# A block-sparse attention kernel with a feed-forward part: value products over the whole array, and the first V transfers regrouped

## The chip, the cores and the metric

One Trainium2 chip, and one of its cores. The metric is device time in microseconds of one execution. The kernel before has a median of 317.98 us over three runs (316.88 to 318.97). The profiled execution took 316.81 us, of which 315.0 us lie between its first and its last instruction (the span).

The engines are named as in the profile: PE (matrix products; PEld is its loading of weights), DVE (vector), ACT (scalar), POOL (GpSimd), SP (the engine that only issues transfers here). "SPq" and the like are the engines' own queues of instructions.

## What is computed

```
q, k, v: (4, 8, 768, 64) fp32; sampled_blocks: (24, 3) int64; block = 32, 24 blocks
scores = q k^T / 8, kept where |qblock - kblock| <= 1, or qblock or kblock is 0 or 23,
         or kblock is one of sampled_blocks[qblock]; elsewhere -1e9
attn   = softmax(scores);  y = attn v
x      = y laid out as (4*768, 8*64)
h      = x @ w_in            (512 -> 2048)
out    = (h * sigmoid(beta * h)) @ w_out     (2048 -> 512), fp32
```

## The kernel before

**Attention.** The 22 inner query blocks of each of the 4 batches are taken two at a time: 11 pairs per batch, 44 pairs `n`. A pair works on 8 key blocks per query block: 3 sampled, block 0, 3 neighbours (the block itself and one on each side), block 23. Query block 0 and 23, which see all keys, are done apart ("global rows", `gs`, `gm`, `ge`, `gn`, `gt`, `gav`).

For a pair, in order: `kg` (POOL) copies the 3+3 sampled key blocks into `KG`, at addresses read from `offP`; `kn` (POOL or DVE) copies the neighbours' keys; `sc` (PE, lines 658 and 668) makes the scores in row- and column-tiled products; `mx` (DVE, L679) and `ex` (ACT, L687) do maximum and exponential; `rc`, `nrm` (POOL, L699) divide by the sum; `tp` (PE, L711) transposes the probabilities with 8 products of 128x128; `ptv` (DVE, L715) moves them to `PT`; `av` (PE, L727) multiplies with the pair's value rows in `VG`; `xv` (DVE or ACT, lines 259 and 261) moves the result, transposed, to `xT`.

In `av` the 128 rows of a stationary operand are 4 key blocks of V (c = 0: sampled blocks and block 0; c = 1: neighbours and block 23), and its 64 columns one head of 64. Two heads `u` lie side by side in the array as two column tiles. That is 2 query blocks x 4 head pairs x 2 x 2 = 32 products with 32 columns moving each, into 256 columns of one PSUM bank.

**Value rows.** `VG` has four buffers; a pair's buffer holds 2 x 2 x 512 values on 128 partitions. V in fp16 is first written to a table in DRAM (`VT`, transfers `vtab`), and the buffers are filled from it by transfers on SP's queue (`vg`, L627): the neighbours' rows (96 partitions, 192 KB), the sampled blocks (six of 32 KB, at addresses read by `vv`), and blocks 0 and 23 (two of 64 KB, on partitions 96 to 127) where the buffer is fresh. Of the first four pairs the sampled rows come from PE instead: `pick` (L638) multiplies V, already on chip, with a selection matrix, and `pickv` moves the result. For the first pairs of a later batch, `vres` copies the rows of blocks 0 and 23 from another buffer on chip.

**Weights.** w_in and w_out come in 8 transfers of 256 KB each on POOL's queue (`win`, `wout`, L461 and L467). A tiny POOL copy, `touch` (L447), reads the first half of batch 0's V and holds them back until it has landed. The transfers of batch 1's V, K and Q follow the last of them on the same queue (L491).

**Feed-forward part.** The tokens are cut into 8 groups of 256 or 512. Per group: 16 tiles `h` (PE, L868, four 128x128 products each), `tanh` (ACT, L874), `stt` (DVE, L879), then `y` (PE, L896). They fill PE between the pieces of attention. The first group needs all of w_in and the results of the first four pairs.

**The order** of every engine's instructions is fixed before launch: class `Plan` simulates the engines with the durations given to `add(...)` and always takes the ready task with the lowest `prio`. So a changed duration or dependency can change the order everywhere. A task's name is its kind and its pair or group.

**Start.** Batch 0's K, Q and V come in six transfers of 768 KB on SP's queue; DVE casts K and Q to fp16, PE transposes them (L508), ACT and DVE move them to `KT` and `QT`; `vperm0` (DVE) makes V's fp16 rows. The sampled block numbers come first (`sbl`, L291), with a step of two words, since they are int64; a mask is built from them on DVE.

Of the kernel before, what the change touches and what calls it, by code (L numbers as in the profile page):

```python
# [22 lines left out]
class Task:  # L23
    def __init__(self, name, eng, dur, emit, deps=(), prio=0.0, lat=0.0,
                 opens=(), closes=(), moe=False, dma=0.0, slack=0.0, hw=0, bulk=None):
        self.on = {eng: dur} if isinstance(eng, str) else dict(eng)
        self.name, self.eng, self.dur, self.emit = name, None, None, emit
        self.deps = [d for d in deps if d is not None]
        self.prio, self.lat = prio, lat
        self.opens, self.closes, self.moe, self.dma = opens, closes, moe, dma  # L30
        self.slack, self.hw, self.bulk = slack, hw, bulk
        self.kind = name.rstrip("0123456789.")
        self.end = None


class Plan:


    HOP = 0.18

    def __init__(self, n_banks, moe_banks):
# [9 lines left out]
    def run(self):  # L51
# [17 lines left out]
        lanes = [0.0] * 8  # L69
        issued = 0  # L70

        bank_free = [(0.0, i) for i in range(self.n_banks)]
# [15 lines left out]
        while done < len(tasks):  # L88
            progress = False
            for e in engines:  # L90
# [3 lines left out]
                for t in waiting[e]:  # L94
                    if ready_at[t] > now + 1e-9:
                        continue
                    if len(t.on) > 1:
                        cost = {o: max(free[o], now) + d + BIAS.get((t.kind, o), 0.0)
                                for o, d in t.on.items()}
                        if cost[e] > min(cost.values()) + 1e-9:  # L100
                            continue
                    if t.bulk is not None and ring_at > now + t.bulk + 1e-9:
                        continue
                    if t.opens:
                        n_ok = sum(1 for f, _ in bank_free if f <= now + 1e-9)
                        if n_ok < len(t.opens):
                            continue
                        if t.moe and attention_left and held_moe + len(t.opens) > self.moe_banks:
                            continue
                    if best is None or t.prio < best.prio:  # L110
                        best = t
# [3 lines left out]
                for other in t.on:  # L115
                    waiting[other].remove(t)
                t.eng, t.dur = e, t.on[e]
                if t.opens:
                    bank_free.sort()
                    for name in t.opens:  # L120
                        _, i = bank_free.pop(0)
                        self.bank[name] = i
                        if t.moe:
                            held_moe += 1
                            moe_owner.add(name)
                    if not t.moe:
                        attention_left -= 1
# [55 lines left out]
def kernel(  # L183
# [11 lines left out]
    nc = tc.nc  # L195
# [19 lines left out]
    def sb(name, shape, dt=FP16):  # L215
        return pool.tile(shape, dt, name=name)

    NKG, NVG, NP, NPT, NT, NO, NG = 3, 4, 3, 2, 3, 3, 2
    NSEL = 4
    PK, GSB = 0.6, 5  # L220

    SR, SG0, SN, SG1 = 0, 3, 4, 7
# [14 lines left out]
    KG = [sb(f"KG{i}", [P, 2, NHP, 8 * BLK]) for i in range(NKG)]  # L237
    VG = [sb(f"VG{i}", [P, 2, 2, D_MODEL]) for i in range(NVG)]
    PP = [sb(f"PP{i}", [P, 2, 2, 8 * BLK]) for i in range(NP)]
# [30 lines left out]

    sbl = sb("sbl", [1, NB, 3], I32)
    ctx_nc = nc
# [14 lines left out]
    def emit_sbl():  # L287
        src = sampled_blocks.tensor
        import dataclasses
        h = dataclasses.replace(src, shape=[NB, 6], dtype=I32)  # L290
        nc.scalar.dma_start(out=sbl, in_=bass.AP(tensor=h, offset=0, ap=[[0, 1], [6, NB], [2, 3]]))  # L291
    t_sbl = add("sbl", "ACT", 0.5, emit_sbl, prio=-200, dma=0.3, hw=1)

# [11 lines left out]
    def emit_idx():  # L305
        V = nc.gpsimd
        V.tensor_copy(out=sf, in_=sbl[:, 1:NB - 1, :])
        for t, m in ((offP, 16.0), (offV, 32.0)):
            V.tensor_scalar(out=t[:, :, 0:6], in0=sf[:, :, :].rearrange("o (p g) r -> o p (g r)", g=2),
                            scalar1=m, scalar2=1.0, op0=ALU.mult, op1=ALU.mult)  # L310
# [120 lines left out]
    for i, (nm, t, dst) in enumerate((("K", k, RK), ("Q", q, RQ), ("V", v, None))):  # L431
        for f in range(2):
            tl = add(f"ld{nm}0.{f}", "SP", 0.47, lambda i=i, t=t, f=f: nc.sync.dma_start(
                out=stage_half(i, f) if i < 2 else v_stage[:, f * HH:(f + 1) * HH, :],
                in_=src6(t, 0, f * HH, HH)), prio=-80 + i * 2 + f, dma=2.0, hw=1)
            if nm == "V":
# [12 lines left out]

    tch = touch(w_in_sb[0:1, 0, 0:1], v_stage[0:1, 0, 0:1], v0ld[0], -58)  # L450

# [6 lines left out]
    for c in range(4):  # L458
        for f in range(2):
            ps = slice(64 * f, 64 * f + 64)  # L460
            t_win.append(add(f"win{c}.{f}", "POOL", 0.6, lambda c=c, ps=ps: nc.gpsimd.dma_start(  # L461
                out=w_in_sb[ps, c, :], in_=w_in_r[c, ps, :]),
                deps=[tch], prio=-50 + 0.2 * c + 0.1 * f, dma=1.3, bulk=THR))
    for c in range(4):
        for f in range(2):
            ps = slice(64 * f, 64 * f + 64)
            t_wout.append(add(f"wout{c}.{f}", "POOL", 0.6, lambda c=c, ps=ps: nc.gpsimd.dma_start(  # L467
                out=w_out_sb[ps, 4 * c:4 * c + 4, :].rearrange("x i m -> x (i m)"), in_=w_out_r[c, ps, :]),
                deps=[tch], prio=-49 + 0.2 * c + 0.1 * f, dma=1.3, bulk=THR))

# [6 lines left out]
    for b in range(B):  # L477
# [24 lines left out]
        for nm, s16, dstT, tr, ev in (("K", RK, KT, trK, evK), ("Q", RQ, QT, trQ, evQ)):  # L502
            for hp in range(NHP):
                def emit_tr(nm=nm, s16=s16, b=b, hp=hp):
                    o = bank16((nm, b, hp))
                    for j in range(J):
                        for u in range(2):
# [3 lines left out]
                                identity=identity, tile_position=(0, u * D))  # L511
                tr[b, hp] = add(f"tr{nm}{b}.{hp}", "PE", 0.36, emit_tr, deps=[ld[nm, b, hp], t_ident],
                                prio=pr + hp, lat=0.2, opens=((nm, b, hp),))
# [34 lines left out]
    for n, (b, p) in enumerate(order_pairs):  # L548
# [5 lines left out]
        first_v = n < NVG or order_pairs[n - NVG][0] != b  # L554
        head_v = p == 0 or n < NSEL
        kt32 = KT[b % 2][:, :, :].bitcast(FP32)
# [32 lines left out]
        kdeps = [evK[b, hp] for hp in range(NHP)] + ([sc[n - NKG]] if n >= NKG else [])  # L589
        kg[n] = add(f"kg{n}", "POOL", 1.15, emit_kg, deps=[t_idx] + kdeps, prio=pr)  # L590
        kn[n] = add(f"kn{n}", {"POOL": 0.5 + 0.6 * first_k, "DVE": 0.45 + 0.25 * first_k}, None,
# [11 lines left out]
        def moves(n=n, vgb=vgb, vt=vt, i0=i0, first=head_v):  # L603
            if first:
                for c, blk in enumerate((0, NB - 1)):
# [3 lines left out]
                                ap=[[D_MODEL, BLK], [0, 2], [1, D_MODEL]]))  # L609
            if i0 + 1 < NB - 2:  # L610
                yield 0.6, lambda v: (
# [12 lines left out]
        for k_, (cost, f) in enumerate(moves()):  # L624
            def emit_vg(n=n, f=f):
# [4 lines left out]
                             prio=pr, dma=cost, hw=1))  # L630


        picked = []
# [12 lines left out]
        if first_v and not head_v:  # L646
            def emit_vres(eng, vgb=vgb, src=VG[(n - p) % NVG]):
                o, i = vgb[3 * BLK:P, :, :, :], src[3 * BLK:P, 0:1, :, :]
                copy_on(eng, o, i.to_broadcast([BLK, 2, 2, D_MODEL]))
            vres = add(f"vres{n}", {"POOL": 2.1, "DVE": 0.62}, None, emit_vres,  # L650
                       deps=vg[n - p] + ([av[n - NVG]] if n >= NVG else []), prio=pr)

        def emit_sc(n=n, b=b, p=p, i0=i0, kgb=kgb):
# [11 lines left out]
            for g in range(2):  # L665
                for hp in range(NHP):
                    for u in range(2):
# [5 lines left out]
                            tile_position=(u * D, hp * BLK))  # L673
        sc[n] = add(f"sc{n}", "PE", 0.46, emit_sc,
                    deps=[kg[n], kn[n], t_mask] + [evQ[b, hp] for hp in range(NHP)], prio=pr, lat=0.2,
# [42 lines left out]

        def emit_av(n=n, vgb=vgb):
            o = bank(("O", n))  # L720
            pt = PT[n % NPT].rearrange("x (g c u m) -> x g c u m", g=2, c=2, u=2)
            for g in range(2):
                for hp in range(NHP):
                    for c in range(2):
                        for u in range(2):
                            us = slice(u * D, (u + 1) * D)
# [5 lines left out]
                                tile_position=(0, u * D))  # L732
        av[n] = add(f"av{n}", "PE", 0.47, emit_av, deps=[ptv[n], vres] + vg[n] + picked, prio=pr - 0.5, lat=0.2,
                    opens=(("O", n),))
        def emit_xv(eng, n=n, b=b, i0=i0):
            c0 = x_of(b * NB + i0)
            copy_on(eng, xT[:, :, c0:c0 + 2 * BLK].rearrange("x h (g m) -> x g h m", g=2),
                    bank(("O", n))[:, 0:2 * NHP * BLK].rearrange("x (g h m) -> x g h m", g=2, h=NHP))
        evs = [add(f"xv{n}", {"DVE": 0.42, "ACT": 0.38}, None, emit_xv, deps=[av[n]], prio=pr - 0.5,
                   closes=(("O", n),))]  # L740
        for g in range(2):
# [6 lines left out]
    for b in range(B):  # L748
        for w, (blk, u) in enumerate((bl, u) for bl in (NB - 1, 0) for u in range(2)):
# [15 lines left out]
            if u == 0:  # L765
                gs = add(f"gs{m}", "PE", 0.5, emit_gs, deps=([mx[GSB + w, 1]] if b == 0 else []) + [evK[b, hp] for hp in range(NHP)] +
                         [evQ[b, hp] for hp in range(NHP)], prio=pr, lat=0.2,
# [27 lines left out]
            def emit_gt(m=m, pg=pg):  # L795
                o = bank16(("GT", m))
                pj = pg[:, :].rearrange("x (p j) -> x j p", j=J)
                for j in range(J):
                    nc.tensor.transpose(out=o[:, j * P:(j + 1) * P], in_=pj[:, j, :], identity=identity)
            gt[m] = add(f"gt{m}", "PE", 0.44, emit_gt, deps=[gn[m]], prio=pr, lat=0.2, opens=(("GT", m),))  # L800
            gptv[m] = add(f"gptv{m}", "DVE", 0.47, lambda m=m, w=w: nc.vector.tensor_copy(  # L801
# [5 lines left out]
        def emit_gav(b=b):  # L807
            o = bank(("GO", b))
            for hp in range(NHP):
                for j in range(J):  # L810
                    for u in range(2):
# [6 lines left out]
                            tile_position=(0, u * D))  # L818
        gavt[b] = add(f"gav{b}", "PE", 1.4, emit_gav, deps=[gptv[gun - 4 + w] for w in range(4)] +
                      vperm[b], prio=pr, lat=0.2, opens=(("GO", b),))  # L820
# [134 lines left out]
```

## Time and profile before

| | us |
|---|---|
| median of three runs | 317.98 |
| lowest, highest | 316.88, 318.97 |
| profiled execution, whole | 316.81 |
| its span, first to last instruction | 315.0 |
| PE busy | 291.3 (92%) |
| DVE busy | 232.1 (74%) |
| ACT busy | 212.4 (67%) |
| POOL busy | 185.4 (59%) |

A row of the list of groups reads: source line, engine, operation, output from inputs, shapes, count; then the busy time of the group (overlapping instructions counted once), the mean ns of one, and the idle time of the engine right before them with what ended it. A row of a timeline reads: start in us, duration in us, engine, line, operation, count of merged instructions; products are pipelined, so that the next row can start before the last one ends, and the distance of two starts is what a group takes. A row of the table by stretches of time gives, for each engine, its busy time and its instructions, then the granted clock of PE, the share of the transfer engines and GB/s.

### The profile page before, as it was taken

The page shows a single profiled execution, that of the slowest core. Times are in us where ns is not written, and L with a number is a line of the kernel's source. Part 1 is how long each engine was busy: PE and PEld are TensorE (multiplying, and loading weights), DVE is VectorE, ACT ScalarE, POOL GpSimd, SP SyncE. Part 2 cuts the span into 40 slices and gives each one's busy share as a digit, 9 for nine tenths or more (in the row PEclk, how much of TensorE's full clock was granted, in tenths as well). Part 3 has the DMA queues.
Part 4 walks back from the last instruction along what each step waited for, and adds up shares of the span by engine and source line. Part 5 has one row for each costly group of instructions (what it writes and reads, how often), then busy time and mean ns, then how long its engine had stood idle before and what let it go on. Part 6 is the DMA issues. An engine that isn't in the chain of part 4 may idle for free.

```text
span 315.0 us, 12633 instructions
## 1 busy us (share of the span) xinstructions
PE 291.3 (92%) x4569; PEld 179.8 (57%) x4569; DVE 232.1 (74%) x536; ACT 212.4 (67%) x625; POOL 185.4 (59%) x534
## 2 busy tenths in 40 slices
PE   0889869998989899999999999999999999999994
PEld 0645558756946676556556565545655555554671
DVE  2972785988899999999985478999679845670160
ACT  1753757875876989778785579857679835671361
POOL 3389985988388797599687354648836842200000
PEclk9999956999999999999999999999999999999999
DMA  7969999699976886345899752234233341100201
GB/s 248 354 138 209 218 212 194 125 202 248 204 152 133 250 151 137 109 129 100 151 171 242 175 152 77 67 115 109 83 90 90 84 138 49 35 1 33 100 2 67
DMA packets 41546, 43.70 MB, mean 139 GB/s; under 512 B 6152, under 2 KB 37000, under 8 KB 41484
## 3 DMA queue, kind: packets, MB, share of 16 engines
q1 hardware_dynamic: 27088, 25.32, 27.8%
q0 software_dynamic: 10784, 11.27, 24.1%
q10 hardware_dynamic: 3612, 6.30, 5.5%
q8 instruction: 36, 0.59, 0.8%
q14 instruction: 26, 0.21, 0.2%
HBM read 44.70 MB, written 9.44 MB: 172 GB/s over the span
## 4 chain that ended last, share of the span: by engine, by line
PE 68%; DMA 7%; DVE 7%; issue 5%; POOL 4%; SPq 3%; POOLq 1%; ACT 1%; DVEq 0%; ACTq 0%
PE bank L868 23%; PE bank L896 22%; PE bank L727 7%; PE bank L711 6%; DMA RQ<-in_q_dram 6%; PE bank L668 2%; SPq L627 2%; PE bank L658 2%; POOL KG L566 2%; PE bank L508 2%; DMA VG<-VT 1%; PE bank L638 1%; DVE SG L773 1%; POOLq L561 1%; DVE ST L679 1%
## 5 line engine op out<-in xcount | busy, mean ns | idle before, releaser
L699 POOL TENSOR_SCALAR PP<-PP,ST 128x256 f16<-128x256 f16 x176 | 83.5, 490 | 35.7 <-DVE ST L693 31.1
L868 PE MATMUL bank<-xT,w_in_sb 128*128 128x256 f16 (+1 forms) x512 | 94.9, 332 | 1.9 <-DVE g L879 1.3
L687 ACT ACTIVATE PP<-bank,ST 128x256 f16<-128x256 f32 x176 | 81.6, 485 | 17.5 <-DVE ST L679 14.3
L896 PE MATMUL bank<-w_out_sb,g 128*128 128x512 f16 x384 | 91.3, 380 | 0.8 <-DVE g L879 0.8
L874 ACT ACTIVATE t<-bank,beta_sb 128x512 f16<-128x512 f32 (+1 forms) x128 | 70.0, 595 | 18.6 <-PE bank L868 15.5
L879 DVE SCALAR_TENSOR_TENSOR g<-t,bank 128x512 f16<-128x512 f16 (+1 forms) x128 | 66.4, 547 | 19.6 <-ACT t L874 19.2
L566 POOL COPY KG<-KT 128x64 f32 x264 | 53.9, 253 | 34.1 <-PE bank L668 26.7
L868 PEld LDWEIGHTS <-w_in_sb 128*128 128x128 f16 x512 | 54.2, 115 | 26.5 <-issue 4.8
L679 DVE TENSOR_REDUCE ST<-bank 128x2 f32<-128x512 f32 x88 | 57.3, 680 | 10.7 <-PE bank L668 10.6
L896 PEld LDWEIGHTS <-g 128*128 128x128 f16 x384 | 34.7, 98 | 39.2 <-issue 4.5
L715 DVE COPY PT<-bank 128x1024 f16<-128x1024 f16 x44 | 30.2, 685 | 14.1 <-PE bank L711 13.6
L687 ACT ACTIVATION_READ_ACCUMULATOR PP<-bank,ST 128x1 f32 x176 | 38.2, 217 | 0.0
L727 PEld LDWEIGHTS <-VG 128*64 128x64 f16 x1408 | 27.4, 115 | 17.3 <-issue 13.1
L727 PE MATMUL bank<-PT,VG 128*64 128x32 f16 x1408 | 31.5, 186 | 4.3 <-issue 2.1
L265 ACT ACTIVATE osb<-bank 128x512 f32<-128x512 f32 x24 | 14.4, 599 | 22.8 <-PE bank L896 22.7
L711 PE MATMUL bank<-identity,PP 128*128 128x128 f16 x352 | 28.4, 225 | 0.5 <-DVE PTG L801 0.3
L711 PEld LDWEIGHTS <-PP 128*128 128x128 f16 x352 | 23.0, 100 | 7.6 <-POOL PP L699 0.9
L780 ACT ACTIVATE PG<-bank,SG 128x384 f16<-128x384 f32 x32 | 18.3, 578 | 5.2 <-DVE ST L693 2.3
L668 PE MATMUL bank<-KG,QT 64*32 64x256 f16 x704 | 18.8, 278 | 0.9 <-POOL KG L566 0.8
L791 POOL TENSOR_SCALAR PG<-PG,SG 128x768 f16<-128x768 f16 x14 | 13.2, 946 | 9.4 <-ACT PG L780 3.8
L259 ACT CAST xT<-bank 128x256 f16<-128x256 f32 x25 | 9.5, 381 | 12.8 <-PE bank L727 11.0
L773 DVE TENSOR_REDUCE SG<-bank 128x1 f32<-128x384 f32 x32 | 16.1, 546 | 0.6 <-PE bank L759 0.5
(94 smaller groups left out, 261.7 us busy)
## 6 DMA issues: line engine op xcount, KB each, us to landing
VG<-VT SPq DMA_DIRECT2D x244, 32.0 KB, 2.8
VG<-VT SPq DMA_DIRECT2D x40, 192.0 KB, 3.8
out_dram<-osb ACTq DMA_DIRECT2D x20, 256.0 KB, 2.2
RV<-in_v_dram POOLq DMA_DIRECT2D x6, 384.0 KB, 5.8
RK<-in_k_dram POOLq DMA_DIRECT2D x6, 384.0 KB, 6.3
RQ<-in_q_dram POOLq DMA_DIRECT2D x6, 384.0 KB, 6.0
VT<-Vn SPq DMA_DIRECT2D x3, 768.0 KB, 6.0
w_in_sb<-in_moe_w_in_dram POOLq DMA_DIRECT2D x8, 256.0 KB, 8.0
```

The lines of the kernel that those rows point to most:

```text
L566: nc.gpsimd.tensor_copy(out=kg32[:, g, :, (SR + r) * W:(SR + r + 1) * W], in_=kt32[:, :, bass.ds(vals[3 * g + r], W)])
L668: nc.tensor.matmul(bk[u][hp * BLK:(hp + 1) * BLK, g * 256:(g + 1) * 256], lhsT=QT[b % 2][u * D:(u + 1) * D, hp, (i0 + g) * BLK:(i0 + g + 1 ...
L679: mx[n, u] = add(f"mx{n}.{u}", "DVE", 0.6, lambda n=n, u=u, sb_=sb_: nc.vector.tensor_reduce(out=sb_[:, 0, 2 * u:2 * u + 2], in_=bank(("S" ...
L687: nc.scalar.activation(out=pb[:, u, g, :], in_=bank(("S", n, u))[:, g * 256:(g + 1) * 256], func=AF.Exp, bias=sb_[:, 0, 2 * u + g:2 * u + ...
L699: (nc.vector if eng == "DVE" else nc.gpsimd).tensor_scalar(out=pb[:, u, g, :], in0=pb[:, u, g, :], scalar1=sb_[:, 2, 2 * u + g:2 * u + g + ...
L711: nc.tensor.transpose(out=o[:, s * P:(s + 1) * P], in_=pb[:, u, g, c * P:(c + 1) * P], identity=identity)
L715: ptv[n] = add(f"ptv{n}", "DVE", 0.61, lambda n=n: nc.vector.tensor_copy(out=PT[n % NPT], in_=bank16(("T", n))), deps=[tp[n]] + ([av[n - N ...
L727: nc.tensor.matmul(o[us, (g * NHP + hp) * BLK:(g * NHP + hp + 1) * BLK], lhsT=vgb[:, g, c, (2 * hp + u) * D:(2 * hp + u + 1) * D], rhs=pt[ ...
L868: nc.tensor.matmul(o[:, 0:TW], lhsT=w_in_v[:, c, f // 4, f % 4, :], rhs=xT[:, c, c0:c0 + TW], start=(c == 0), stop=(c == NHP - 1))
L874: lambda G=G, f=f, TW=TW, tt=tt: nc.scalar.activation(out=tt[:, 0:TW], in_=bank(("H", G, f))[:, 0:TW], func=AF.Tanh, bias=0.0, scale=beta_ ...
L879: lambda G=G, f=f, TW=TW, tt=tt, gg=gg: nc.vector.scalar_tensor_tensor(out=gg[:, f, 0:TW], in0=tt[:, 0:TW], scalar=1.0, in1=bank(("H", G, ...
L896: nc.tensor.matmul(o[:, :], lhsT=gg[:, f, s * P:(s + 1) * P], rhs=w_out_sb[:, f, :], start=(f == 0), stop=(f == N_FFC - 1))
```

## The change

Five parts:

1. `av` uses the whole array: one stationary operand is 128 rows by the 128 columns of two heads, and both heads' probabilities (2 x 32 columns) move through it. 16 products of 64 columns take the place of 32 of 32 columns. Half of each result, the products of one head's values with the other's probabilities, is not used; the result takes all 512 columns of the bank.
2. `xv` becomes two copies on 64 partitions each (one per head of the pair), since the wanted halves lie in different columns. Each may go to DVE or ACT.
3. The four `VG` buffers become one tile, `VGs`, and the neighbours' rows of pairs 0 to 3 come in one transfer of 768 KB (96 partitions x 8 x 512). Blocks 0 and 23 are transferred for pair 0 only; pairs 1 to 3 get them by `vres`. `av` of pairs 0 to 3 waits for all of pair 0's transfers.
4. Of the weights only the first two transfers follow `touch`, which now reads the second half of batch 0's V; the other 14 follow `touch2`, which reads the end of the 768 KB transfer.
5. The block numbers are fetched as 144 words in a row, and every second one is read on chip.

Besides, the planner is told other durations, and that PE takes 0.1 us more where the tiling of the array changes from one task to the next.

```diff
+    TILING = {"sc": 1, "gs": 1, "av": 2, "gav": 2, "trK": 2, "trQ": 2}
+    CHANGE, KEEP = 0.1, 0.0
...
+                if e == "PE" and t.tiling != tiling:
+                    t.dur += self.CHANGE
+                    tiling = t.tiling
...
+    EARLY = 1
+    WIDE = 0
...
-    VG = [sb(f"VG{i}", [P, 2, 2, D_MODEL]) for i in range(NVG)]
+    VGs = sb("VG", [P, NVG, 2, 2, D_MODEL])
+    VG = [VGs[:, i, :, :, :] for i in range(NVG)]
...
-        nc.scalar.dma_start(out=sbl, in_=bass.AP(tensor=h, offset=0, ap=[[0, 1], [6, NB], [2, 3]]))
+        nc.scalar.dma_start(out=sbl, in_=bass.AP(tensor=h, offset=0, ap=[[0, 1], [6, NB], [1, 6]]))
...
-    tch = touch(w_in_sb[0:1, 0, 0:1], v_stage[0:1, 0, 0:1], v0ld[0], -58)
+    tch = touch(w_in_sb[0:1, 0, 0:1], v_stage[0:1, HH, 0:1], v0ld[1], -58)
+    tch2 = add("touch2", "POOL", 0.6, lambda: nc.gpsimd.tensor_copy(
+        out=w_in_sb[0:1, EARLY, 0:1], in_=VGs[0:1, 0, 0, 1, 0:1]), prio=-57.5)
...
-                deps=[tch], prio=-50 + 0.2 * c + 0.1 * f, dma=1.3, bulk=THR))
+                deps=[tch if c < EARLY else tch2], prio=-50 + 0.2 * c + 0.1 * f, dma=1.3, bulk=THR))
...
-        head_v = p == 0 or n < NSEL
+        head_v = p == 0
...
-            if i0 + 1 < NB - 2:
+            if n < NSEL:
+                if n == 0:
+                    yield 2.2, lambda v: (
+                        VGs[0:3 * BLK, 0:NSEL, :, 1, :].rearrange("x n g m -> x (n g) m"),
+                        bass.AP(tensor=vt.tensor, offset=vt.offset, ap=[
+                            [D_MODEL, 3 * BLK], [BLK * D_MODEL, 2 * NSEL], [1, D_MODEL]]))
+            elif i0 + 1 < NB - 2:
...
+        if n == 0:
+            tch2.deps.append(vg[0][-1])
...
+                        if wide:
+                            nc.tensor.matmul(
+                                o[:, (g * NHP + hp) * 2 * BLK:(g * NHP + hp + 1) * 2 * BLK],
+                                lhsT=vgb[:, g, c, hp * P:(hp + 1) * P],
+                                rhs=pt[:, g, c, :, hp * BLK:(hp + 1) * BLK],
+                                start=(g + hp + c == 0), stop=(c == 1), skip_group_check=True)
+                            continue
...
+        for u in range(2 if wide else 1):
+            def emit_xv(eng, n=n, b=b, i0=i0, u=u, wide=wide):
+                c0 = x_of(b * NB + i0)
+                if wide:
+                    us = slice(u * D, (u + 1) * D)
+                    src = bank(("O", n))[us, :].rearrange("x (g h v m) -> x g h v m", g=2, h=NHP, v=2)[:, :, :, u, :]
...
+                copy_on(eng, xT[us, :, c0:c0 + 2 * BLK].rearrange("x h (g m) -> x g h m", g=2), src)
```

## The prediction

> **What bounds the kernel now.** I read the table by stretches of time first, then the list of groups, then PE's timeline in a steady stretch.
>
> ```profile
> core 0: us, PE busy (x) PEld busy (x) DVE busy (x) ACT busy (x) POOL busy (x), PEclk, DMA share, GB/s
> 0.00:56.00 56.00, 42.07 (x622) 28.63 (x623) 35.23 (x99) 31.08 (x93) 38.82 (x110) 0.88 0.94 224
> 56.00:80.00 24.00, 22.56 (x464) 15.68 (x463) 20.94 (x56) 17.86 (x58) 20.87 (x62) 1.00 0.97 192
> 80.00:160.00 80.00, 75.95 (x1518) 51.05 (x1512) 76.24 (x179) 66.42 (x207) 61.18 (x170) 1.00 0.68 150
> 160.00:280.00 120.00, 120.00 (x1819) 66.78 (x1814) 89.81 (x183) 83.98 (x245) 64.49 (x195) 1.00 0.41 108
> 280.00:315.00 35.00, 30.75 (x175) 17.71 (x172) 9.86 (x22) 13.04 (x27) 0.00 (x0) 1.00 0.13 46
> ```
>
> From 160 us until its last product PE never rests: there every us of PE work is a us of time. From 80 to 160 PE rests 4.05 us, but DVE only 3.76: two limits side by side. Before 56 us it is a chain of waits, with transfers near their full share (0.94).
>
> ```profile
> L896 PEld LDWEIGHTS <-g 128*128 128x128 f16 x384 | 34.7, 98 | 39.2 <-issue 4.5
> L727 PEld LDWEIGHTS <-VG 128*64 128x64 f16 x1408 | 27.4, 115 | 17.3 <-issue 13.1 <-DMA VG<-VT 3.9
> L727 PE MATMUL bank<-PT,VG 128*64 128x32 f16 x1408 | 31.5, 186 | 4.3 <-issue 2.1 <-DVE ST L693 1.9 <-DVE PT L715 0.3
> L261 DVE CAST xT<-bank 128x256 f16<-128x256 f32 x23 | 9.7, 420 | 7.4 <-PE bank L727 6.1 <-PE bank L813 0.9
> L259 ACT CAST xT<-bank 128x256 f16<-128x256 f32 x25 | 9.5, 381 | 12.8 <-PE bank L727 11.0 <-DVE SG L773 1.1 <-POOL PP L699 0.5
> ```
>
> The value products hold PE for 31.5 us; these two kinds of eviction are what doubles (four of the 48 belong to the global rows).
>
> ```profile
> 225.06 1.03 PE L868 MATMUL bank<-xT,w_in_sb 128*128 128x512 f16 x4
> 226.02 0.68 PE L727 MATMUL bank<-PT,VG 128*64 128x32 f16 x32
> 226.63 0.62 PE L711 MATMUL bank<-identity,PP 128*128 128x128 f16 x8
> 227.09 1.03 PE L868 MATMUL bank<-xT,w_in_sb 128*128 128x512 f16 x4
> 227.96 0.61 PE L711 MATMUL bank<-identity,PP 128*128 128x128 f16 x8
> 228.40 1.03 PE L868 MATMUL bank<-xT,w_in_sb 128*128 128x512 f16 x4
> 229.36 1.19 PE L727 MATMUL bank<-PT,VG 128*64 128x32 f16 x64
> 230.48 0.28 PE L658 MATMUL bank<-maskr,ones 64*32 64x192 f16 x8
> ```
>
> Distances of starts: 32 value products and what follows them take 226.63-226.02 = 0.61, 64 take 1.12; so 32 take 0.51 (32 ns for a pair of column tiles), and 0.10 more go once, on leaving. Four L868 products take 0.96 ahead of value products and 0.87 ahead of transposes: entering costs 0.09. So where the tiling of the array changes, PE loses about 0.095.
>
> **1. Products over the whole array.** What bounds one new product? Its 64 columns: L868 takes 0.87/4 = 218 ns for 512 columns and, at the end of the chain of waits, 6.99/64 = 109 ns for 256, so 0.42 ns a column and 29 ns for 64 with the remainder of about 2 ns. Or its weights: 128 columns are loaded for each, and no row has such products with so few columns moving. The nearest is L711: the same size of weights with 128 columns moving, 0.44 to 0.46 for eight, 56 ns each. So a pair costs between 16 x 29 = 0.46 and 16 x 56 = 0.90, for 0.51 now. I take 0.46: contiguous 128x128 weights (L896) are recorded with 98 ns, less than the 128x64 ones of now (115), so the wider load is not the longer one. In the built orders, from the first product of the feed-forward part on, 39 value steps follow (40 before, one moved ahead) and PE changes tiling 111 times instead of 166. Sum: 55 x 0.095 = 5.2 and 39 x 0.05 = 2.0, together **-7.2**; upper end 39 x 0.39 - 5.2 = +10.0. Of the 7.2, 4.3 (32 changes, 25 steps) fall behind the first product of group 3 at about 140 us, where only PE counts. The first five steps earn nothing: there PE waits.
>
> By the Trainium skill, page "TensorEngine Tiling (Array Packing)", section "When to Use Tiling", column tiling for a stationary operand of at most 64 columns is worth up to 2x. By that rule a pair would go from 0.51 to 1.02, and the sum to 39 x 0.51 - 5.2 = +14.7; L711's 56 ns for 128 columns leave room for at most 0.90.
>
> By the Trainium skill, page "TensorE: Matmul & The Clock Gate", section "LDWEIGHTS (loading the stationary operand)", a load takes columns / 1.2 ns, 107 for 128. Where loads set the pace that would be 1.7 us a pair; L711 contradicts it, with a new 128-column load every 56 ns.
>
> **2. Evictions.** 88 copies of 64 partitions x 256 replace 44 of 128 x 256; elements per partition are the same, so I take the same 0.42 (DVE) and 0.38 (ACT); below nothing they can't be, above it at most the same again for the strided source. The order gives DVE 46 instead of 20 and ACT 42 instead of 24: +10.9 and +6.8 us. Behind 160 us DVE and ACT idle 30 and 36 of 120 us, which covers them. Between the first DVE products of groups 1 and 3 (81 to 142 us) DVE gets 13 copies instead of 5, +3.4, and kn, vres and KT/QT copies shuffled by the new order add about 0.6; its cover is the 3.76 idle. Queued behind a late copy are `mx`, `ptv` and `stt`, and PE's next step behind those. Between 0 and +4.0 I take **+2.0**.
>
> **3. Front of the start.** `sbl` is issued at 0.74 and POOL has it at 6.06; masks then hold DVE until the first cast at 8.06, though K's first half, issued at 0.75, landed 4.8 us later. Words in a row instead of 72 single ones: at worst no gain; at best it lands so early that all mask work is over before the cast, 8.06-6.3 = 1.7. The second half of K lands at 1.26+6.8 = 8.06 anyhow and V at 16.4, so part is taken back: **-1.3**, from 0 to -1.7.
>
> **4. V in one transfer, weights behind it.** Now the neighbours' transfers of pairs 0 to 3 are issued at 22.41, 23.84, 26.84 and 30.67 and land 6.0, 8.1, about 11 and 12.4 us later, among weight transfers. PE waits for them: 1.38 within av1, and 0.93, 0.94 and 0.74 at av2 and av3 (other names stand there, but VG's were the later semaphores): 4.0 us. Afterwards the 768 KB go out at about 22.4, beside 128 KB of V and two weight transfers only; at the 210 GB/s of this stretch 1.4 MB take 6.7, so they land at about 29 (6.0 us for 768 KB of VT at best, 12.4 at worst: 28.4 to 34.8). av0 comes up on PE at about 33, behind seven picks, so nothing waits. Nine issues of about 0.45 leave SP's queue. `vres` of pairs 1 to 3 costs DVE 3 x 0.75, between 24 and 35 us; DVE is busy 1.97 of 8 us from 24 to 32.
>
> What pays for it: `touch2` stands on POOL behind nrm0, kg5 and nrm2, at about 31; behind it four weight transfers (0.55 each), then kg6, which waits for sc3, and in the new order sc3 stands behind av2 (about 36). So the last of w_in goes out at about 41 instead of 33.75, and lands 5 to 8.6 us later (the times of its like), 46 to 49.5; the first feed-forward product now starts at 47.76. The 4.0 us are thus mostly handed on to this wait and to the scores of pairs 3 to 6, which ACT's exponentials (0.91 each, two a pair) follow in a row from 37 on. What stays: pairs 5 to 7 are further, and DVE and ACT owe less in group 0. Between -4.0 and +1.7 I take **-1.0**.
>
> **Sum.** 316.8 - 7.2 + 2.0 - 1.3 - 1.0 = 309.3 on the profiled run; the median stands 317.98/316.81 = 1.0037 above that: **310.5**.
>
> **Rivals** (each times 1.0037).
>
> A, *the weight load sets the pace*: 56 ns a product, 316.8 + 10.0 + 2.0 - 2.3 = 326.5, so **327.7**, slower; it decides from 41 ns a product on (16 x 41 = 0.65 = 0.51 + (5.2 + 0.3) / 39, where 0.3 is what the start earns beyond the evictions). For: no row shows such products; a 64-column pair now needs 32 ns though only 32 columns move, so the load may already be the limit. Against: 98 to 115 ns above. Chance 0.10. By the Trainium skill's tiling rule above it would be 332.4.
>
> B, *DVE becomes the bound until 142 us*: the 2.9 us of PE gain ahead of group 3 are lost, and with no slack left DVE adds its 4.0 less the idle 3.8; I keep +2.0. 316.8 - 4.3 + 2.0 - 1.3 = 313.2 with the start's gain lost too, **314.4**; with the whole 4.0, 316.4. For: 95% busy. Against: ACT has 13.6 us idle there. 0.15.
>
> C, *weights late*: if the 768 KB need 12.4 us, POOL stands at `touch2` until 34.8; the last of w_in goes out at 44.7, lands at 52 and the first feed-forward product is 4 to 5 us late, and PE's granted clock, 0.50 from 40 to 48 us, may stay low 1.7 us' worth longer: 309.3 + 1.0 + 6.2 = 316.5, **317.7**. 0.10.
>
> D, *the start keeps its gain*: the 4.0 us at av1 to av3 all stay: 306.3, **307.4**. 0.10.
>
> Forecast, 307.5 to 314.5: 0.55.
>
> **How the numbers follow.** Runs of this kernel spread 0.7%, so 1% (3.2 us) is what can be told. Below 314.8 lie the forecast (0.55), D (0.10) and a third of B (0.05): 0.70 faster. The rest of B and 0.07 of C: 0.17 within. A and 0.03 of C: 0.13 slower. The range takes in D, B and half of C: 304.5 to 317.
>
> **What would show it.** Right: the new value step's busy time falls from 31.5 to about 21 us with starts 29 ns apart, L868 before it takes 0.87, and the last product of the chain ends 6 to 8 us earlier. Wrong: starts 40 ns or more apart (A); DVE above 97% and PE idle above 6 us from 80 to 160 (B); a wait of the first L868 product for w_in, or a second low-clock stretch (C).

## The result, and the profile after

| | before | after |
|---|---|---|
| median, us (8 runs each) | 316.55 | 321.09 |
| ratio to before, 95% interval | | 1.0104 (1.0061 to 1.0148) |
| profiled execution / span, us | 316.81 / 315.0 | 321.01 / 319.2 |
| PE, DVE, ACT busy, us | 291.3, 232.1, 212.4 | 286.6, 244.8, 218.2 |

The changed kernel is 1.0% slower, 3.3 us, where 7.5 us of gain were forecast. The medians take in every execution, but the ratios, here and below, leave out those in which the kernel ran in a slower state (over 1.5% above its fastest), so a ratio can differ from that of two medians. The table by stretches of time of the changed kernel, columns as in the prediction:

```profile
core 0: us, PE busy (x) PEld busy (x) DVE busy (x) ACT busy (x) POOL busy (x), PEclk, DMA share, GB/s
0.00:56.00 56.00, 40.99 (x557) 28.67 (x557) 42.55 (x116) 34.70 (x105) 39.39 (x124) 0.88 0.88 221
56.00:80.00 24.00, 22.23 (x386) 15.77 (x386) 20.97 (x54) 18.30 (x56) 15.93 (x35) 1.00 0.99 194
80.00:160.00 80.00, 70.04 (x1184) 48.04 (x1180) 70.18 (x172) 63.18 (x199) 57.26 (x163) 0.98 0.63 136
160.00:280.00 120.00, 118.44 (x1556) 66.85 (x1555) 98.10 (x196) 85.48 (x256) 73.70 (x215) 1.00 0.44 114
280.00:319.20 39.20, 34.88 (x194) 19.90 (x192) 13.03 (x26) 16.54 (x32) 0.00 (x0) 1.00 0.11 41
```

From 80 to 160 us both engines that were nearly full before now rest: PE 9.96 us (4.05 before) and DVE 9.82 (3.76). Nothing is saturated there; the engines wait for each other. What they don't do there comes after 280 us, where PE has 34.9 us of work left instead of 30.8. The list of groups, shapes apart:

```profile
L756 PE MATMUL bank<-PT,VG 128*128 128x64 f16 x704 | 29.0, 196 | 4.9 <-DMA VG<-VT 3.1 <-DVE PT L742 1.0 <-ACT PP L714 0.4
L756 PEld LDWEIGHTS <-VG 128*128 128x128 f16 x704 | 26.5, 100 | 14.6 <-issue 9.1 <-DMA VG<-VT 0.4
L277 DVE CAST xT<-bank 64x256 f16<-64x256 f32 x46 | 19.4, 421 | 13.3 <-PE bank L756 7.1 <-ACT xT L275 5.4
L275 ACT CAST xT<-bank 64x256 f16<-64x256 f32 x42 | 15.4, 366 | 14.1 <-PE bank L756 10.3 <-DVE xT L277 3.4
```

A half copy costs what a whole one did (421 and 366 ns). New is the end of the two copy rows: where the halves of a pair stand on different engines, the second waits for the first (8.8 us in 16 waits).

PE's timeline of after shows the new value step in a steady stretch:

```profile
228.82 1.04 PE L942 MATMUL bank<-w_out_sb,g 128*128 128x512 f16 x4
229.70 0.63 PE L756 MATMUL bank<-PT,VG 128*128 128x64 f16 x16
230.26 0.95 PE L859 MATMUL bank<-PTG,Vn 128*64 128x64 f16 x48
```

```profile
121.77 0.63 PE L756 MATMUL bank<-PT,VG 128*128 128x64 f16 x16
122.23 0.60 PE L914 MATMUL bank<-xT,w_in_sb 128*128 128x256 f16 x4
```

Four full-array products take 0.88 ahead of the value step: entering costs nothing now. From start to start the step takes 0.56 ahead of tiled products, and 0.46 to 0.47 where the next operation uses the whole array, 29 ns a product. So the pace of the products is what was forecast.

The same timeline has PE's waits (in brackets: idle time and what ended it). Those of over 0.9 us between 90 and 192 us:

```profile
97.51 0.61 PE L738 MATMUL bank<-identity,PP 128*128 128x128 f16 x8 [1.79 <-ACT PG L826]
104.80 0.49 PE L845 MATMUL bank<-identity,PG 128*128 128x128 f16 x6 [0.97 <-DVE g L925]
117.61 1.35 PE L526 MATMUL bank<-identity,RK 128*64 128x128 f16 x24 [2.67 <-DMA RK<-in_k_dram]
144.65 0.61 PE L738 MATMUL bank<-identity,PP 128*128 128x128 f16 x8 [1.03 <-ACT PP L714]
```

With 1.29 us for a Q transfer at 79.6 these are five waits and 7.75 us from 56 to 192. Before has one, for the same transfer:

```profile
78.35 0.86 PE L508 MATMUL bank<-identity,RQ 128*64 128x128 f16 x24 [1.06 <-DMA RQ<-in_q_dram]
```

How far the kernel has come is read from the start of the first feed-forward product on DVE (`stt`) of groups 0 to 7:

| us | 0 | 1 | 2 | 3 | 4 | 5 | 6 | 7 | end |
|---|---|---|---|---|---|---|---|---|---|
| before | 49.8 | 80.8 | 104.8 | 141.6 | 185.6 | 227.1 | 269.9 | 298.5 | 315.0 |
| after | 53.7 | 75.8 | 104.3 | 148.4 | 191.8 | 234.4 | 275.4 | 302.6 | 319.2 |

After is 5 us ahead at group 1, level at group 2, and 6.8 behind at group 3; from there it wins 2.6 back. The two rows for group 3, before and after:

```profile
141.60 0.67 DVE L879 SCALAR_TENSOR_TENSOR g<-t,bank 128x512 f16<-128x512 f16 x1
148.42 0.66 DVE L925 SCALAR_TENSOR_TENSOR g<-t,bank 128x512 f16<-128x512 f16 x1
```

### The profile page after: what moved, and what is told of

Same layout as the page of the kernel before. It is cut to its first block, busy times and chain, and to the rows that moved or that the text cites. A ratio compares the mean times of both kernels' runs of the same rounds, so it can differ in the third digit from the quotient of the medians.

```text
span 319.2 us, 11244 instructions
## 1 busy us (share of the span) xinstructions
PE 286.6 (90%) x3865; PEld 179.2 (56%) x3865; DVE 244.8 (77%) x562; ACT 218.2 (68%) x645; POOL 186.3 (58%) x536
## 4 chain that ended last, share of the span: by engine, by line
PE 43%; DMA 20%; DVE 18%; ACT 9%; issue 4%; POOL 3%; SPq 2%; ACTq 0%; POOLq 0%; DVEq 0%
PE bank L914 17%; PE bank L942 14%; DMA VG<-VT 7%; DMA RQ<-in_q_dram 5%; DVE ST L706 4%; PE bank L756 4%; DVE g L925 3%; ACT PP L714 3%; DVE SG L819 3%; DMA RK<-in_k_dram 3%; PE bank L738 3%; ACT t L920 3%; DMA g<-in_q_dram 2%; DMA VT<-Vn 2%; SPq L651 2%
## 5 line engine op out<-in xcount | busy, mean ns | idle before, releaser
L726 POOL TENSOR_SCALAR PP<-PP,ST 128x256 f16<-128x256 f16 x168 | 81.6, 501 | 48.1 <-DVE ST L720 44.8
L914 PE MATMUL bank<-xT,w_in_sb 128*128 128x256 f16 (+1 forms) x512 | 96.0, 333 | 1.3 <-DVE g L925 0.4
L584 POOL COPY KG<-KT 128x64 f32 x264 | 52.9, 250 | 24.4 <-PE bank L695 12.1
L714 ACT ACTIVATION_READ_ACCUMULATOR PP<-bank,ST 128x1 f32 x176 | 37.0, 211 | 0.0
L756 PEld LDWEIGHTS <-VG 128*128 128x128 f16 x704 | 26.5, 100 | 14.6 <-issue 9.1
L738 PE MATMUL bank<-identity,PP 128*128 128x128 f16 x352 | 29.2, 227 | 5.6 <-ACT PG L826 1.8
L756 PE MATMUL bank<-PT,VG 128*128 128x64 f16 x704 | 29.0, 196 | 4.9 <-DMA VG<-VT 3.1
L738 PEld LDWEIGHTS <-PP 128*128 128x128 f16 x352 | 23.8, 102 | 13.9 <-POOL PP L726 4.2
L277 DVE CAST xT<-bank 64x256 f16<-64x256 f32 (+1 forms) x48 | 20.2, 421 | 13.3 <-PE bank L756 7.1
L275 ACT CAST xT<-bank 64x256 f16<-64x256 f32 (+1 forms) x44 | 16.1, 367 | 14.2 <-PE bank L756 10.3
```

The lines of the kernel that those rows point to most:

```text
L277: (nc.vector if eng == "DVE" else nc.gpsimd).tensor_copy(out=out, in_=in_)
L584: nc.gpsimd.tensor_copy(out=kg32[:, g, :, (SR + r) * W:(SR + r + 1) * W], in_=kt32[:, :, bass.ds(vals[3 * g + r], W)])
L714: nc.scalar.activation(out=pb[:, u, g, :], in_=bank(("S", n, u))[:, g * 256:(g + 1) * 256], func=AF.Exp, bias=sb_[:, 0, 2 * u + g:2 * u + ...
L726: (nc.vector if eng == "DVE" else nc.gpsimd).tensor_scalar(out=pb[:, u, g, :], in0=pb[:, u, g, :], scalar1=sb_[:, 2, 2 * u + g:2 * u + g + ...
L738: nc.tensor.transpose(out=o[:, s * P:(s + 1) * P], in_=pb[:, u, g, c * P:(c + 1) * P], identity=identity)
L756: nc.tensor.matmul(o[:, (g * NHP + hp) * 2 * BLK:(g * NHP + hp + 1) * 2 * BLK], lhsT=vgb[:, g, c, hp * P:(hp + 1) * P], rhs=pt[:, g, c, :, ...
```

## The experiments

Ratios are to the kernel before on the same chip, with 95% intervals. "Order" is the planner's order of every engine, with its choice of engine for the tasks that two engines can do. Each theory's expectation stands ahead of its result.

**First set: products, copies or the new order?** Theory O: the new order makes the loss. Theory E: the doubled copies do.

`wide_same_order`: before, with its order; products as in the change, both half copies on the engine that had the one.

```diff
-                        for u in range(2):
-                            nc.tensor.matmul(o[us, ...], lhsT=vgb[:, g, c, (2 * hp + u) * D:(2 * hp + u + 1) * D], ...)
+                        nc.tensor.matmul(o[:, ...], lhsT=vgb[:, g, c, hp * P:(hp + 1) * P], rhs=pt[:, g, c, :, hp * BLK:(hp + 1) * BLK], ...)
...
-            copy_on(eng, xT[:, :, c0:c0 + 2 * BLK]..., bank(("O", n))[:, 0:2 * NHP * BLK]...)
+            for u in range(2):
+                copy_on(eng, xT[us, :, c0:c0 + 2 * BLK]..., bank(("O", n))[us, :]...)
```

> The kernel before, with its order and its banks left as they are; only the value products go over the whole array and each eviction becomes two copies of half the partitions, one behind the other on the engine that had the one. Theory O (the loss comes from the new order; the products themselves gain): 310 to 314 against 316.5 before, value steps 0.47 us each, PE idle from 80 to 160 us at most 1.5 us above the 4.05 of before. Theory E (the doubled evictions eat the gain, in whatever order): 316 or more, PE idle from 80 to 160 us 7 us or more.

315.44 us, 0.9943 (0.9907 to 0.9980): products and copies together gain 0.6% in before's order. But the time lies between the two expectations, and so does PE's rest from 80 to 160 us, 6.86 us, nearer to E's mark. PE's work fell by 6.6 us over the kernel, but its rest in 56 to 280 us rose by 6.1.

`narrow_new_order`: after, in its order, with the products of before and one copy; the second copy's place in the order is empty.

> The changed kernel in its own order, with the value products and the single eviction of before put back in their places (the second eviction of each pair is empty). Theory O: the stall between 104 and 148 us stays, and the narrower products cost 3 to 7 us on top: 323 to 328. Theory E: fewer evictions, so 314 to 318, and the stall is gone.

324.81 us, 1.0179 (1.0111 to 1.0246). Group 3 comes at 149.1, so the stall stays, and E's time is missed by far: taking the new products and the second copies out doesn't heal the new order. Whether they help in that order isn't shown, since the interval overlaps that of after.

`start_only`: after with `WIDE = 99`, `CHANGE = 0` and the durations of before, so only the start's parts and the order planned for them.

> The changed kernel with narrow value products and the planner's old durations: only the transfers of the start, the weights behind them and the block numbers are new; the order is planned anew. Theory O: the start's gain of up to 4 us is kept or lost as this third order has it, 313 to 319, with the first product of the feed-forward part no later than 49 us. Theory S (the late weights cost): first feed-forward product at 50 us or later and 319 to 323.

317.93 us, 1.0043 (1.0002 to 1.0084), in O's range, with the first feed-forward product at 46.9. It is 2.8 us ahead of before at group 3 (138.8) and 0.6 behind at group 4 (186.3).

`hoist`: the 2.67 us wait for K in after comes from a transfer that POOL issues behind two normalisations (`gn6`, `gn7`); here `ldK2.1` stands ahead of `gn4`, `ldQ2.0` and `ldQ2.1` ahead of `gn5` and `gn6`.

> The changed kernel, with three transfers of batch 2 (second half of K, both halves of Q) taken ahead of three to four steps of the global rows on POOL's queue; the rest of the order is kept. Theory O: the 2.7 us wait of PE for K at 115 us and the low clock behind it (3.4 us at half rate, 1.7 us) go: 316 to 318 against 321. Theory E: K's wait hides others, so at most 1 us is won: 320 to 321.

321.80 us, 1.0072 (1.0025 to 1.0119), not to be told from after; O's 316 to 318 is missed. The wait for K is gone, and PE's timeline has another instead:

```profile
100.35 1.01 PE L738 MATMUL bank<-identity,PP 128*128 128x128 f16 x8 [5.04 <-ACT PG L826]
```

So taking this wait away doesn't win the loss back.

**Second set: which part made the order bad, and what do the copies cost?** Theory P: PE is only one of several engines that set the pace. Theory S: the weights held back.

`after_old_costs` is after with the durations of before (`CHANGE = 0`, `sc` 0.46, `av` 0.47, `gs` 0.5, `gt` 0.44, `gav` 1.4 ...):

> The whole change, but its order planned with the kernel before's durations (scores 0.46, value products 0.47, global scores 0.50, global transposes 0.44, global values 1.40, nothing for a change of tiling). Theory O (the order planned with the new durations makes the stall of 104 to 148 us): the first feed-forward product of group 3 on VectorE comes by 141, not 148.4, and the time is 314 to 317. Theory S (the held-back weights and V's one transfer make it): group 3 still at 146 or later, time 319 to 322. Theory P (TensorE was only one of several engines that set the pace, so its saving turns into waits wherever it is made): like O at group 3, but TensorE idle 4 us or more above before in 24 to 280 us, time 315 to 318.

`no_start` is after with the start of before (parts 3 to 5 undone):

> The whole-array value products with two copies and all of the planner's new durations, but the start as before: the strided fetch of the indices, V's rows one transfer a pair, all weights behind the first V half. Theory O: the stall stays, group 3 at 146 or later, time 318 to 322. Theory S: no stall, time 313 to 316.

`evict_twice`:

```diff
-            copy_on(eng, xT[:, :, c0:c0 + 2 * BLK]..., bank(("O", n))[:, 0:2 * NHP * BLK]...)
+            for u in range(2):
+                copy_on(eng, xT[us, :, c0:c0 + 2 * BLK]..., bank(("O", n))[us, 0:2 * NHP * BLK]...)
```

> The kernel before in its own order with its 64-column value products; only the copy of each pair's values is made in two halves of 64 partitions, one behind the other on the same engine. Theory E (46 more copies of 0.38 to 0.42 us each are on the path): ratio 1.008 to 1.02, 319 to 323 us. Theory P (each engine has slack that covers its share, and the price falls in waits that are there): ratio 1.000 to 1.006.

`wide_one_copy`:

```diff
+                        nc.tensor.matmul(o[:, ...], lhsT=vgb[:, g, c, hp * P:(hp + 1) * P], ...)
...
+            copy_on(eng, xT[:, :, c0:c0 + 2 * BLK]..., bank(("O", n))[:, :].rearrange("x (g h v m) -> x g h v m", ...)[:, :, :, 0, :])
```

> The kernel before in its own order with whole-array value products and one copy of 128 partitions a pair, which takes the columns of the even heads for all partitions: the odd heads' values aren't taken from their own columns. It does as many copies as the kernel before and has the shorter products. Theory E (the second copy ate the gain): 308 to 312 us, ratio 0.97 to 0.985. Theory P: ratio 0.987 to 0.996, TensorE's idle time in 56 to 280 us still 4 us or more above before's 5.4.

| | median, us | ratio |
|---|---|---|
| after_old_costs | 321.08 | 1.0107 (1.0052 to 1.0162) |
| no_start | 322.42 | 1.0110 (1.0059 to 1.0162) |
| evict_twice | 322.70 | 1.0162 (1.0116 to 1.0207) |
| wide_one_copy | 311.50 | 0.9843 (0.9778 to 0.9909) |

Neither the durations nor the start is the cause by itself: with either taken back the loss stays (group 3 comes at 148.5 in `after_old_costs` and at 145.0 in `no_start`), so O as I had put it (the new durations make the bad order) fell, and S with it. E holds: the copies alone (44 more, not the 46 of the expectation) cost 1.6%, 5.1 us, and the products without them gain 1.6%, 5.0 us. P's times fit neither run, though one mark of P is there: in `wide_one_copy` PE rests 9.6 us in 56 to 280, 4.1 more than in before.

The table by stretches tells where the copies cost. First `evict_twice`, then `wide_one_copy`:

```profile
80.00:160.00 80.00, 71.77 (x1376) 47.89 (x1374) 72.97 (x174) 62.95 (x199) 56.21 (x157) 0.98 0.64 142
160.00:280.00 120.00, 119.08 (x1854) 66.32 (x1852) 95.60 (x196) 87.19 (x260) 69.22 (x207) 1.00 0.44 113
```

```profile
80.00:160.00 80.00, 73.87 (x1248) 48.41 (x1247) 76.81 (x180) 67.14 (x210) 62.74 (x175) 1.00 0.72 150
160.00:280.00 120.00, 119.24 (x1501) 67.21 (x1500) 90.13 (x182) 83.52 (x240) 62.51 (x186) 1.00 0.39 104
```

With more to do, DVE is busy less from 80 to 160 us in `evict_twice` (72.97, before 76.24), because it waits longer for the other engines. This trace is of the slowest of four executions (323.85 us). In it 6.4 us are lost between groups 1 and 3 (67.2 against 60.8), some 1.7 of them in 3.4 us at half clock that before doesn't have there (mean clock 0.98). Only 1.6 are lost from group 3 to 7 (158.5 against 156.9), though from 160 to 280 us DVE does 5.8 us more, in a stretch in which PE stays nearly full (119.08 of 120).

**Third set: is any new order this bad?** Theory X: the waits between the halves on two engines are the order's price. Theory R: every newly planned order costs 4 to 5 us against that of before.

`joined`: both halves one task, `{"DVE": 0.84, "ACT": 0.76}`, otherwise after.

> The changed kernel, but the two half copies of a pair are one task on one engine, planned at 0.84 us on VectorE or 0.76 on ScalarE, so that no half waits for the other on the other engine (16 such waits and 8.8 us in the changed kernel's trace). Theory X (those waits between the halves are what the new order costs): ratio 0.994 to 1.000, time 315 to 318. Theory R (every newly planned order costs about 4 to 5 us against the order of before, whatever made the planner move): ratio 1.006 to 1.014, time 319 to 322.

`shake_hop20` and `shake_hop16`: before with one number of the planner changed.

```diff
-    HOP = 0.18
+    HOP = 0.20
```

> The kernel before with its own work; only the planner's time for a hand-over between engines is 0.20 us in place of 0.18, which gives another order of the same instructions. Theory X: ratio 0.997 to 1.005. Theory R: ratio 1.008 to 1.02, 320 to 324 us.

> The same with 0.16 us. Theory X: ratio 0.997 to 1.005. Theory R: ratio 1.008 to 1.02. If the two differ by over 1% in either direction, an order's worth is chance to that amount.

`costs_only`: `no_start` with `WIDE = 99`.

> The kernel before with its own work (64-column value products, one copy a pair, its own start), its order planned with the change's durations and its 0.1 us for a change of tiling. Theory X: ratio 0.997 to 1.005. Theory R: 1.008 to 1.02. A third theory, that measured durations give the better order: below 0.99.

| | median, us | ratio | group 4 at, us |
|---|---|---|---|
| joined | 323.32 | 1.0211 (1.0123 to 1.0299) | 193.7 |
| shake_hop20 | 321.84 | 1.0185 (1.0090 to 1.0279) | 191.0 |
| shake_hop16 | 324.00 | 1.0228 (1.0145 to 1.0311) | 192.5 |
| costs_only | 323.77 | 1.0274 (1.0189 to 1.0359) | 190.9 |

Theory R has the direction right, but only `shake_hop20` lies in its range; the other three lose more than it said. X and the third theory fell. The same operations, planned with 20 ns more or less for a hand-over, run 1.9 and 2.3% slower (the plan also shifts some between engines: VectorE has 20 of the 48 copies to `xT`, 23 in before). The loss is there by group 4 (185.6 in before). In the two shaken orders much of it is rest of PE: 9.4 and 10.0 us from 56 to 192 us, against 5.5 in before and 12.4 in after; a mean clock of 0.98 from 80 to 160 us (before 1.00) adds some 1.6 us (0.02 of 80). The longest wait of `shake_hop20`, then of `shake_hop16`:

```profile
138.77 0.61 PE L711 MATMUL bank<-identity,PP 128*128 128x128 f16 x8 [2.89 <-ACT PP L687]
```

```profile
141.54 0.49 PE L799 MATMUL bank<-identity,PG 128*128 128x128 f16 x6 [2.38 <-ACT PP L687]
```

What the waits between the halves cost stays open: `joined` has none, and is no faster than after; but it has an order of its own, so their price can't be read from it.

**Fourth set: the parts in the order of before.** Theory R as above; rival Q: before's order is good only for before's work, or the start's parts lose by themselves. `graft` has all parts, both copies on one engine; its order is a written list: `start_only`'s for the planned first 30 us, then before's. `lie` has the same instructions in `start_only`'s order. `index_wide` is `wide_same_order` with part 5; `index_wide_late` has the wide form there only `if n >= 24`. `graft_narrow` and `graft_late` are `graft` with the wide form for no pair, and from 24 on.

> All of the change's parts (whole-array products with both copies on one engine, the contiguous index fetch, V's one transfer, the weights behind it), with the changed start's own order for the planned first 30 us and from there on the order and engines of before. Theory R (the loss is the new order's; the parts themselves gain): ratio 0.975 to 0.992, 309 to 314 us, group 3's first feed-forward product on VectorE by 140. Rival Q (the order of before is good only with before's work and start; or the start's parts lose by themselves): ratio 0.998 to 1.015.

> The change's parts in the order that the planner makes when it is told of the old durations and of one copy of the old price (the order of the run start_only, 1.0043), both half copies behind each other on one engine. Theory R: what the whole-array products save in a given order, 0.6 to 1.6%, comes off that: ratio 0.988 to 0.999. Rival Q: 1.000 to 1.010.

> The kernel before in its own order with whole-array products, two copies on one engine, and the contiguous index fetch; V's transfers and the weights as before. Against wide_same_order (0.9943) the prediction's front term of 1.3 us would give 0.990; if the front's gain is lost behind it, 0.994; Theory R: 0.985 to 0.993.

> The same, but whole-array products and two copies only for the pairs from 24 on (from about 160 us, where TensorE is never idle in before), the 64-column form and one copy ahead of that. If the doubled copies cost most where VectorE is busy 95% (104 to 160 us) and little behind it, this is the best of all: ratio 0.980 to 0.990. If they cost the same everywhere, it is 0.991 to 0.996, behind index_wide.

> graft with the 64-column products and one copy a pair throughout: the start's parts alone, their own order for the planned first 30 us and before's behind it. If the start's parts gain the forecast 2.3 us: ratio 0.990 to 0.995. If they gain nothing where the order of before follows: 0.997 to 1.003. If they lose: above 1.003.

> graft with whole-array products and two copies only for the pairs from 24 on. If the start's parts gain, it is ahead of index_wide_late: ratio 0.980 to 0.987. If they don't, 0.988 to 0.993, level with it or behind.

| | median, us | ratio |
|---|---|---|
| graft | 315.38 | 0.9930 (0.9881 to 0.9979) |
| lie | 317.20 | 0.9987 (0.9939 to 1.0035) |
| index_wide | 316.24 | 0.9987 (0.9942 to 1.0032) |
| index_wide_late | 313.20 | 0.9885 (0.9850 to 0.9921) |
| graft_narrow | 315.18 | 0.9897 (0.9845 to 0.9949) |
| graft_late | 316.12 | 0.9929 (0.9892 to 0.9966) |

The work of the change is 1.7% faster in before's order (`graft`) than in its own (1.0104): 5.5 us, and the sign turns. Since `graft` also keeps both copies of a pair on one engine, the 5.5 us are the price of the new order and of the split halves together. It is between R's range and Q's, nearer to R's; group 3 comes at 141.9, not by 140. `lie`, the same work in `start_only`'s order, is in R's range at no change (0.9987), so that order costs only 0.6% against `graft`, with intervals overlapping: not every new order is equally bad. The start's parts alone gain 1.0%, 3.3 us (`graft_narrow`). The gains don't add: with the wide form on top, `graft` and `graft_late` are at 0.993. The index fetch by itself isn't resolved: `index_wide` missed all three expectations, with 0.9987 against 0.9943 without the fetch, intervals overlapping; its trace is of its fastest execution, 312.8 us, so it is not read here.

`index_wide_late` beats both kernels, and on the same chip `index_wide` (0.9885 against 0.9987). Its stretches, beside those of before in the prediction:

```profile
80.00:160.00 80.00, 75.61 (x1453) 48.58 (x1448) 77.07 (x178) 66.50 (x211) 63.03 (x176) 1.00 0.71 150
160.00:280.00 120.00, 119.07 (x1499) 66.94 (x1497) 93.68 (x190) 86.03 (x246) 60.93 (x183) 1.00 0.38 101
```

That the wide form does this isn't shown. This trace, too, is of the fastest execution (310.5 us), and it is 4.2 us ahead of before at group 3 already (137.4 against 141.6), where no product is wide yet. From group 3 to 7, where most of the late wide form lies, it takes 154.7 us against 156.9 in before. `graft_late` takes 154.9 there (its fastest execution too) and `graft_narrow` 156.9, so the late form seems worth about 2 us in its own stretch. Yet over the whole kernel `graft_late` (0.9929) is no faster than `graft_narrow` (0.9897, same chip, intervals overlapping) or `graft` (0.9930).

## Why the prediction was wrong

- **The order, left at nothing: this is the step that failed.** The part-by-part sum priced the edits as if each stood in the order of before. The reordering appears in it only as copies "shuffled by the new order add about 0.6". The runs: three new orders of before's own work cost 1.9 to 2.7%, 5.9 to 8.7 us, and the change's work loses 5.5 us by its own order and its split halves. With products -5.0, copies +5.1 and start -3.3, the measured parts give -3.2 where after has +3.3; the 6.5 between lie in that span of 5.9 to 8.7. This is an estimate, since the parts don't add exactly: `graft`, with all of them, has -2.2, and `wide_same_order`, with products and copies, -1.8 where their sum is +0.1.
- **Evictions, +2.0 (0 to +4.0)**: +5.1 (3.7 to 6.6). The prices of one copy were right (421 and 366 ns, forecast 0.42 and 0.38). Wrong was to set DVE's 3.76 idle us from 80 to 160 off against the added work as cover: idle time between waits didn't take it up, and in `evict_twice` both engines rested more there (DVE 7.03, PE 8.23 us). "DVE and ACT idle 30 and 36 of 120 us, which covers them" mostly held: 1.6 us behind group 3.
- **Products, -7.2**: mechanism right, the size 5.0 (2.9 to 7.0), just outside. Starts are 29 ns apart, a step takes 0.46 to 0.47, entering is free. By the Trainium skill, page "TensorEngine Tiling (Array Packing)", section "Theoretical Speedup", two tiles are worth up to 2x. With the few moving columns of this kernel the traces show no such gain: 32 ns for a pair of column tiles, 29 for the full-width product that takes its place. "Where only PE counts" behind 140 us held less than forecast: groups 3 to 7 gained 3.0 in `wide_one_copy` (153.9 against 156.9), not 4.3, and PE rests 0.76 us in 160 to 280.
- **The start, -1.3 and -1.0**: together -3.3 (1.6 to 4.9), the sum's -2.3 inside. The K transposes begin at 6.1 instead of 9.2, 3.1 us earlier, more than the 1.7 that I had as the upper end.
- **Rivals.** A fell (29 ns a product). B's mark came by half: PE rests over 6 us in 80 to 160, but DVE is at 88%, not over 97, so it isn't DVE that is the bound. Of C's mark a second stretch of low clock came (117.8 to 121.2 us), behind the wait for K, not for w_in. None of the four had a worse order as its mechanism; being slower was given 0.13 in all, for slower products and late weights.
- **A mark of my own was wrong.** I had the value step's busy time fall to 21 us; it is 29.0, with starts 29 ns apart as forecast. Busy time runs to the modelled end of a step (0.63), not to the next start (0.46 to 0.47).

Open: which property makes the order of before good, and whether its planner's settings had been chosen for it. Its trace has fewer long PE waits ahead of 192 us than the new orders', but `evict_twice` has waits of 1.52 and 2.73 us in that same order, and removing after's longest one moved the time by nothing that could be measured. Not tried: the half copies as two tasks with before's order, which would price the waits between them (16 and 8.8 us in after).

## What to carry to other kernels

Where a planner decides the order, first measure what a new order of the unchanged work costs (here 1.9 to 2.7%); an edit's gain has to be larger than that, or has to be made in the old order. Idle time of an engine in a stretch where several engines hand work round is not cover: by one trace the doubled copies cost 6.4 us there and 1.6 where PE alone was full. So try such an exchange, shorter products for more copies, first in the stretch where the engine that pays has time left; here it won about 2 us in that stretch, but no run shows that it made the whole kernel faster by itself.

## What the hardware showed that was not expected

In after's table by stretches, the 3.4 us before and the 3.4 us of the second low clock:

```profile
114.40:117.80 3.40, 0.73 (x33) 0.41 (x32) 3.12 (x8) 2.01 (x9) 3.34 (x9) 1.00 1.25 230
117.80:121.20 3.40, 3.40 (x39) 2.79 (x35) 0.38 (x1) 2.85 (x8) 3.39 (x13) 0.50 1.15 176
```

PE was busy 0.73 of 3.40 us, not idle, and the granted clock still halved for the next 3.4. The Trainium skill, page "TensorE: Matmul & The Clock Gate", section "What's actually happening", has the length of that window, 3413 ns, and an idle window as the condition; the trace agrees on the length, and shows that a window 21% busy can be enough. `evict_twice` has a second case: PE busy 0.67 us of the 3.4 from 104.6 to 108.0, and a clock of 0.50 from there to 111.4. Which busy share is the limit no run shows. Over a whole run the clock told little: `wide_one_copy` took 311.2 us with a mean granted clock of 0.998 and 310.9 with 0.975.
